# x transposed by the DMA crossbar from chunk 3 on, and a new order of a slot's work, in a windowed attention with a maxout FFN

## The chip, the cores and the metric

The kernel runs on one core of a Trainium2 chip (trn2). The metric is the device time of one execution in microseconds, the lower the better. Times of parts come from one profiled execution.

## The reference

Attention over a window of 128 positions plus four sink positions, and then a feed-forward block that takes the maximum of three products. Cut to what matters:

```python
# q, k, v: [B=4, H=8, S=768, D=64] float32
scores = scale * np.matmul(q, k.transpose(0, 1, 3, 2))
keep = (pos[None, :] < 4) | ((rel >= 0) & (rel < 128))     # rel = query - key position
a = softmax(np.where(keep, scores, -1e9))
attn = np.matmul(a, v)
x = attn.transpose(0, 2, 1, 3).reshape(B * S, H * D)       # [3072, 512]
h = np.maximum(np.maximum(x @ w1, x @ w2), x @ w3)         # [3072, 768]
out = h @ w_out                                            # [3072, 512] float32
```

## The kernel before

The 3072 tokens are worked in twelve chunks of 256 tokens (`NCH`), three to a batch (`CPB`). A chunk goes through these steps, each written as a short token in strings that `run` (L365) reads from left to right; the whole schedule is by hand (`tc.manual_schedule`, L51), so each engine executes its instructions in the order in which the tokens are written.

- `load` (L61): eight DMAs on SP's queue bring Q and K (four of 256 KB, L72) and V (four of 128 KB, L78) as float32. `cast` (L186) turns them into bf16 on POOL.
- D, `turn` (L215): two DMA transposes on SP turn K and Q of a chunk (256 KB each); used from chunk 3 on. K lands in `kT`, Q in `qT`. E, `place_k` (L192), copies `kT` on DVE into the zero-padded `kz`, in two instructions. Chunks 0 to 2 are turned on TensorE (K and Q, `prep`).
- S0 to S7, `score` (L233): for one head two or three matmuls into a PSUM tile `st` (two buffers), then an exponential on ACT (L249); every second head a multiplication by the mask on DVE (L252) for the pair. The chunk that begins a batch has no block before it, so it leaves out L240.
- Z: scores against the sinks and their exponential (L258, L263; the PSUM tile has the tag of `st`), or, on a batch's first chunk, the gathering of the batch's sink keys on DVE (L227).
- A, `av` (L268), for four heads g and 128 tokens t: matmuls with V, then on DVE a reciprocal (L285) and a product (L288) into `x_sb`.
- T0, T1, `xpose` (L293), each for 128 tokens of a chunk: four TensorE transposes of `x_sb` into PSUM (L300) and a copy by ACT into `xT` (L301).
- F0 to F8, `ffn_h` (L306): eight matmuls each with a weight block and all 256 tokens of `xT` (L313). F0, F3 and F6 (the first weight matrix) are cast on ACT into `h_sb` (L317); the others are folded in by a maximum on DVE (L319). Four PSUM buffers.
- Y0, Y1, `ffn_y` (L321): six matmuls for 128 tokens over all of `h_sb` (L324), a copy on ACT (L329), and after Y1 two stores on SP (L336).

From L442 on the loop's pass i, a slot, does D of chunk i+2, the loads and casts of chunk i+3, the attention of chunk i+1 and the feed-forward of chunk i, by this string:

```python
run("Dc", c=i + 2)
if i + 3 < NCH:
    load(i + 3)
    cast(i + 3)
run("Sb0 Fa0 Sb1 Fa1 Sb2 Fa2 Sb3 Fa3 Zb Sb4 Fa4 Ab00 Sb5 Fa5 Ab01 Sb6 Fa6 "
    "Sb7 Fa7 Fa8 Ab10 Ab11 Ec Ya0 Tb0 Tb1 Ya1", a=i, b=i + 1, c=i + 2)
```

Steps on chunks past the last are skipped: slots 9 and 10 load nothing, slot 10 has no D, and slot 11 has only F and Y. SP's queue in a slot is thus: D (two transposes), eight loads, two stores of y.

Of the kernel before, what the change touches and what calls it, by code (L numbers as in the profile page):

```python
# [10 lines left out]
BF16 = mybir.dt.bfloat16  # L11
# [5 lines left out]
def kernel(  # L17
# [13 lines left out]
    nc = tc.nc  # L31
# [10 lines left out]
    CPB = S // 256  # L42
    NCH = B * CPB
    DS = d_model // 128
# [6 lines left out]
    with tc.manual_schedule():  # L51
        const = tc.alloc_tile_pool(name="const", bufs=1)
        raw = tc.alloc_tile_pool(name="raw", bufs=3)
        work = tc.alloc_tile_pool(name="work", bufs=2)
# [6 lines left out]
        def load(ci, gate=None):  # L61

            b, c = divmod(ci, CPB)
            t0 = c * 256
            eng = nc.sync
            qk = raw.tile([128, 2, 2, 512], F32, tag="qk_raw", name="qk_raw")
            vr = raw.tile([128, 2, H, D], F32, tag="v_raw", name="v_raw")
            if gate is not None:
                gate.memset(qk[0:1, 0, 0, 0:1], 0.0)
            for g in range(2):  # L70
                for j, src in ((0, k), (1, q)):
                    eng.dma_start(  # L72
                        out=qk[:, j, g].rearrange("p (h i d) -> p h (i d)", h=4, d=D),
                        in_=src[b, 4 * g:4 * g + 4, t0:t0 + 256]
                            .rearrange("h (p i) d -> p h (i d)", i=2))
            for n in range(2):
                for i in range(2):
                    eng.dma_start(  # L78
                        out=vr[64 * i:64 * i + 64, n],
                        in_=v[b, :, t0 + 128 * n:t0 + 128 * n + 128]  # L80
                            .rearrange("h (p i) d -> i p h d", i=2)[i])
            raws[ci] = (qk, vr)
# [5 lines left out]
        for x in range(n_sink):  # L88
            nc.sync.dma_start(out=vs_raw[x * H:(x + 1) * H],
                              in_=v[:, :, x].rearrange("b h d -> h b d"))  # L90
# [35 lines left out]
        for i in range(2):  # L126
            for slot, op, sign in ((1, ALU.is_ge, 1), (0, ALU.is_gt, -1)):
                m = msk[64 * i:64 * i + 64, slot].rearrange("p (i t) -> p i t", i=2)
                nc.gpsimd.affine_select(
                    out=m, in_=m, compare_op=op, fill=0.0, base=-sign * i,  # L130
# [55 lines left out]
        def cast(ci):  # L186
            for j, g in ((0, 0), (1, 0), (0, 1), (1, 1)):
                cast_qk(ci, j, g, nc.gpsimd)
            for n in range(2):
                cast_v(ci, n, nc.gpsimd)  # L190
# [75 lines left out]
        xs = {}  # L266
# [24 lines left out]
        xTs = {}  # L291

        def xpose(ci, t):  # L293
            if t == 0:
                xTs[ci] = work.tile([128, DS, 256], BF16, tag="xT", bufs=3, name="xT")
            pt = (ps_f.tile([128, DS, 128], BF16, tag="f", name="xt_ps") if ci == 0 else
                  ps_o.tile([128, DS, 128], BF16, tag="o", name="xt_ps"))
            x = xs.pop((ci, t)).rearrange("p h d -> p (h d)")
            for ds in range(DS):
                nc.tensor.transpose(pt[:, ds], x[:, ds * 128:(ds + 1) * 128], ident)  # L300
            nc.scalar.copy(xTs[ci][:, :, t * 128:(t + 1) * 128], pt)  # L301

        hs = {}
        ys = {}
# [1 line left out]
        def ffn_h(ci, n):  # L306
            fp, wi = divmod(n, 3)
            if n == 0:
                hs[ci] = work.tile([128, FB, 256], BF16, tag="h", bufs=3, name="h_sb")
            hp = ps_f.tile([128, 2, 256], F32, tag="f", name="h_ps")  # L310
            for f in range(2):
                for ds in range(DS):
                    nc.tensor.matmul(hp[:, f], lhsT=w_sb[wi][:, ds, (2 * fp + f) * 128:(2 * fp + f + 1) * 128],  # L313
                                     rhs=xTs[ci][:, ds, :], start=(ds == 0), stop=(ds == DS - 1))
            dst = hs[ci][:, 2 * fp:2 * fp + 2]
            if wi == 0:
                nc.scalar.copy(dst, hp)  # L317
            else:
                nc.vector.tensor_max(dst, dst, hp)  # L319
# [18 lines left out]
        def step(op):  # L338

            name, ci, arg = op[0], int(op[1:3]), op[3:]  # L340
            if ci >= NCH:
                return
            if name in "KQ":
                prep(ci, int(name == "Q"), int(arg))
            elif name == "D":
                turn(ci)
            elif name == "E":
                place_k(ci, kTs.pop(ci), slice(0, NP))
            elif name == "S":
                score(ci, int(arg))  # L350
            elif name == "Z":
                if ci % CPB:
                    sink_score(ci)
                elif ci > 0:
                    sink_k(ci // CPB)
            elif name == "A":
                av(ci, int(arg[0]), int(arg[1]))
            elif name == "T":
                xpose(ci, int(arg))
            elif name == "F":  # L360
                ffn_h(ci, int(arg))
            elif name == "Y":
                ffn_y(ci, int(arg))

        def run(text, **at):  # L365
            for tok in text.split():
                c = at[tok[1]]
                step(f"{tok[0]}{c:02d}{tok[2:]}")
# [59 lines left out]
            a=0, b=1, c=2)  # L428
# [13 lines left out]
        for i in range(2, NCH):  # L442
            run("Dc", c=i + 2)
            if i + 3 < NCH:
                load(i + 3)
                cast(i + 3)
            run("Sb0 Fa0 Sb1 Fa1 Sb2 Fa2 Sb3 Fa3 Zb Sb4 Fa4 Ab00 Sb5 Fa5 Ab01 Sb6 Fa6 "
                "Sb7 Fa7 Fa8 Ab10 Ab11 Ec Ya0 Tb0 Tb1 Ya1", a=i, b=i + 1, c=i + 2)

        for pool in (ps_f, ps_o, ps_s, work, raw, const):  # L450
            pool.release()
# [35 lines left out]
```

## Time and profile before

| | |
|---|---|
| median of three runs | 211.01 us (210.33 to 216.31) |
| the profiled execution | 211.01 us, its span 209.2 us |
| mean granted TensorE clock | 0.967 |
| TensorE transposes of x (L300) | 96, 9.5 us busy |
| copies of x on ACT (L301) | 24, 13.2 us busy, 592 ns each |
| maxima (L319) | 72, 49.1 us busy on DVE |
| feed-forward matmuls (L313) | 864, 111.3 us busy |
| DMA transposes K / Q, issue to landing | 4.8 / 3.4 us, nine each |
| loads Q / K / V, issue to landing | 4.6 / 4.1 / 4.2 us |

The profile lists instructions by line and engine. PE is TensorE's matmul, PEld its weight loads, DVE, ACT and POOL the vector, scalar and GpSimd engines, SPq the queue of SyncE, which issues DMAs. "Busy" for matmuls counts overlapping pipeline time, so a row's sum is more than what it holds the array. The chain of waits is followed back from the last instruction, at each step to what released it. The loop's slots 2 to 10 fill the stretch from 61.1 to 193.9 us of the span; ahead of it lies the start with the first two chunks, after it slot 11.

### The profile page before, as it was taken

How to read it: one execution, taken by the hardware profiler on the slowest of the kernel's cores; microseconds unless marked ns; L12 is line 12 of the kernel's file. 1: busy time of each engine (PE TensorE's matmuls, PEld its weight loads, DVE VectorE, ACT ScalarE, POOL GpSimd, SP SyncE). 2: the span in 40 equal slices, each digit the busy share in tenths (PEclk: the TensorE clock that was granted, in tenths of full speed). 3: DMA queues.
4: the chain of work that ended last, by engine and by line, in shares of the span. 5: the costliest groups of instructions: out<-in, count | busy, mean ns of one | idle time of the engine just before them, and what ended most of it. 6: DMA issues, size and time to landing. Idle time of an engine off the chain costs nothing.

```text
span 209.2 us, 4734 instructions
## 1 busy us (share of the span) xinstructions
PE 187.6 (90%) x1895; PEld 149.6 (72%) x1895; DVE 122.8 (59%) x271; ACT 107.4 (51%) x198; POOL 66.6 (32%) x113
## 2 busy tenths in 40 slices
PE   7664598999839999999999999999999999999991
PEld 7544477986427959869779599599597797896860
DVE  4793340887314966737748746747768477375340
ACT  8865244154514556466375375384462853754321
POOL 7355717989005243430340421702402500000000
PEclk9999579999966999999999999999999999999999
DMA  5899995990498999939939969679489580300304
GB/s 147 226 241 197 208 253 105 202 242 1 98 231 210 196 271 189 245 82 200 265 72 151 315 115 223 168 129 278 101 162 261 128 155 3 94 9 0 100 3 100
DMA packets 75749, 33.37 MB, mean 159 GB/s; under 512 B 45776, under 2 KB 72656, under 8 KB 75728
## 3 DMA queue, kind: packets, MB, share of 16 engines
q1 hardware_dynamic: 73344, 29.93, 63.3%
q0 software_dynamic: 2384, 3.15, 8.9%
q8 instruction: 15, 0.25, 0.5%
q14 instruction: 6, 0.05, 0.1%
HBM read 25.20 MB, written 6.29 MB: 151 GB/s over the span
## 4 chain that ended last, share of the span: by engine, by line
PE 68%; DVE 11%; DMA 7%; SPq 6%; ACT 3%; issue 2%; POOL 1%; DVEq 0%; POOLq 0%
PE h_ps L313 43%; PE y_ps L324 8%; PE st L242 4%; PE o_ps L280 4%; DMA v_raw<-in_v_dram 4%; DVE x_sb L288 4%; DVE h_sb L319 4%; SPq L78 3%; DMA kT<-qk_bf 2%; PE st L243 2%; DVE e_sb L252 2%; PE xt_ps L300 2%; SPq L72 2%; PE st L240 1%; PE sk L258 1%
## 5 line engine op out<-in xcount | busy, mean ns | idle before, releaser
L313 PE MATMUL h_ps<-xT,w 128*128 128x256 bf16 x864 | 111.3, 278 | 0.7 <-ACT xT L301 0.7
L313 PEld LDWEIGHTS <-w 128*128 128x128 bf16 x864 | 82.9, 100 | 11.4 <-issue 0.8
L249 ACT ACTIVATE e_sb<-st 128x512 bf16<-128x512 f32 (+1 forms) x96 | 53.4, 564 | 33.7 <-PE st L243 32.8
L319 DVE TENSOR_TENSOR h_sb<-h_sb,h_ps 128x512 bf16<-128x512 bf16 x72 | 49.1, 683 | 22.6 <-PE h_ps L313 20.0
L252 DVE TENSOR_TENSOR e_sb<-e_sb,msk 128x1024 bf16<-128x1024 bf16 (+1 forms) x48 | 32.9, 685 | 40.8 <-ACT e_sb L249 40.6
L180 POOL CAST qk_bf<-qk_raw 128x512 bf16<-128x512 f32 x44 | 28.6, 657 | 86.7 <-DMA qk_raw<-in_k_dram 76.6
L324 PE MATMUL y_ps<-wo,h_sb 128*128 128x512 bf16 x144 | 35.3, 379 | 0.0
L329 ACT COPY y_sb<-y_ps 128x512 f32<-128x512 f32 x24 | 14.1, 586 | 37.5 <-PE y_ps L324 37.5
L242 PE MATMUL st<-qT,kz 128*128 128x256 bf16 x96 | 26.6, 281 | 5.0 <-DVE kz L196 3.9
L317 ACT CAST h_sb<-h_ps 128x512 bf16<-128x512 f32 x36 | 21.1, 586 | 15.7 <-PE h_ps L313 15.6
L243 PE MATMUL st<-qT,kz 128*128 128x128 bf16 x96 | 21.5, 225 | 0.0
L280 PEld LDWEIGHTS <-e_sb 128*128 128x128 bf16 x352 | 17.1, 99 | 6.0 <-issue 3.3
L324 PEld LDWEIGHTS <-h_sb 128*128 128x128 bf16 x144 | 12.3, 98 | 12.7 <-DVE h_sb L319 3.4
L288 DVE TENSOR_TENSOR x_sb<-o_ps,rc 128x256 bf16<-128x256 f32 x48 | 20.4, 424 | 1.6
L280 PE MATMUL o_ps<-ve,e_sb 128*128 128x65 bf16 x352 | 19.2, 196 | 0.9 <-DVE e_sb L252 0.8
L184 POOL CAST ve<-v_raw 128x512 bf16<-128x512 f32 x24 | 16.4, 694 | 10.4 <-DMA v_raw<-in_v_dram 9.9
L242 PEld LDWEIGHTS <-kz 128*128 128x128 bf16 x96 | 9.6, 100 | 6.6 <-issue 4.1
L240 PE MATMUL st<-qT,kz 128*128 128x128 bf16 x64 | 14.3, 223 | 0.0
L301 ACT COPY xT<-xt_ps 128x512 bf16<-128x512 bf16 x24 | 13.2, 596 | 0.4 <-PE xt_ps L300 0.3
L196 DVE COPY kz<-kT 64x1024 bf16<-64x1024 bf16 x18 | 9.9, 550 | 5.5 <-DMA kT<-qk_bf 5.2
L272 PE MATMUL o_ps<-vs,e_sink 128*128 128x260 bf16 x32 | 9.0, 282 | 3.4 <-POOL vs L168 3.4
L300 PE MATMUL xt_ps<-ident,x_sb 128*128 128x128 bf16 x96 | 9.5, 221 | 2.4 <-DVE x_sb L288 1.5
(44 smaller groups left out, 108.0 us busy)
## 6 DMA issues: line engine op xcount, KB each, us to landing
qk_raw<-in_k_dram SPq DMA_DIRECT2D x24, 256.0 KB, 4.1
qk_raw<-in_q_dram SPq DMA_DIRECT2D x24, 256.0 KB, 4.6
v_raw<-in_v_dram SPq DMA_DIRECT2D x48, 128.0 KB, 4.2
out_dram<-y_sb SPq DMA_DIRECT2D x22, 256.0 KB, 3.8
w<-in_moe_w_dram POOLq DMA_DIRECT2D x3, 768.0 KB, 9.4
wo<-in_moe_w_out_dram POOLq DMA_DIRECT2D x2, 384.0 KB, 5.7
out_dram<-y_sb SPq DMA_DIRECT2D x4, 128.0 KB, 2.3
kT<-qk_bf SPq DMA_TRANSPOSE x9, 4.8
```

Of the source, the lines that this page charges most:

```text
L180: eng.tensor_copy(dst.rearrange("p i (h d) -> p h i d", d=D), src)
L184: eng.tensor_copy(ve[b % 2][:, 2 * c + n, :, 0:D], raws[ci][1][:, n])
L242: nc.tensor.matmul(st[:, 1:3], lhsT=kh[:, 0:128], rhs=qh, start=True, stop=True)
L243: nc.tensor.matmul(st[:, 3], lhsT=kh[:, 128:256], rhs=qh[:, 1], start=True, stop=True)
L249: nc.scalar.activation(e[:, h, lo:], st[:, lo:], AF.Exp, scale=scale)
L252: nc.vector.tensor_tensor(out=e[:, :, lo:], in0=e[:, :, lo:], in1=m, op=ALU.mult)
L280: nc.tensor.matmul(o[:, hh], lhsT=es[ci, p][:, h, sl], rhs=ve[b % 2][:, n, 2 * p + h], start=(c == 0 and x == 0), stop=(x == len(blocks) - 1),
L288: nc.vector.tensor_mul(xs[ci, t][:, 4 * g:4 * g + 4], o[:, :, 0:D], rc.unsqueeze(2).to_broadcast([128, 4, D]))
L313: nc.tensor.matmul(hp[:, f], lhsT=w_sb[wi][:, ds, (2 * fp + f) * 128:(2 * fp + f + 1) * 128], rhs=xTs[ci][:, ds, :], start=(ds == 0), stop ...
L317: nc.scalar.copy(dst, hp)
L319: nc.vector.tensor_max(dst, dst, hp)
L324: nc.tensor.matmul(yp, lhsT=hs[ci][:, fb, t * 128:(t + 1) * 128], rhs=wo[:, fb], start=(fb == 0), stop=(fb == FB - 1))
```

## The change

From chunk 3 on, T issues one DMA transpose on SP for each half of x instead of four TensorE transposes and an ACT copy. `xT` is laid out by halves of the tokens for this, and L313 reads it in two runs of 128. The string of the loop is written anew: S1 and S2 and the later scores stand closer together, F4 to F8 come later, T0 and T1 stand directly after A10 and A11, and E stands between F6 and F7. D stands ahead of the slot's loads as it did.

```diff
@@ -292,13 +292,17 @@
 
         def xpose(ci, t):
             if t == 0:
-                xTs[ci] = work.tile([128, DS, 256], BF16, tag="xT", bufs=3, name="xT")
+                xTs[ci] = work.tile([128, 2, DS, 128], BF16, tag="xT", bufs=3, name="xT")
+            if ci >= CPB:
+                nc.sync.dma_start_transpose(
+                    out=xTs[ci][:, t], in_=xs.pop((ci, t)).rearrange("p h d -> p (h d)"))
+                return
             pt = (ps_f.tile([128, DS, 128], BF16, tag="f", name="xt_ps") if ci == 0 else
                   ps_o.tile([128, DS, 128], BF16, tag="o", name="xt_ps"))
             x = xs.pop((ci, t)).rearrange("p h d -> p (h d)")
             for ds in range(DS):
                 nc.tensor.transpose(pt[:, ds], x[:, ds * 128:(ds + 1) * 128], ident)
-            nc.scalar.copy(xTs[ci][:, :, t * 128:(t + 1) * 128], pt)
+            nc.scalar.copy(xTs[ci][:, t], pt)
 
         hs = {}
         ys = {}
@@ -311,7 +315,7 @@
             for f in range(2):
                 for ds in range(DS):
                     nc.tensor.matmul(hp[:, f], lhsT=w_sb[wi][:, ds, (2 * fp + f) * 128:(2 * fp + f + 1) * 128],
-                                     rhs=xTs[ci][:, ds, :], start=(ds == 0), stop=(ds == DS - 1))
+                                     rhs=xTs[ci][:, :, ds], start=(ds == 0), stop=(ds == DS - 1))
             dst = hs[ci][:, 2 * fp:2 * fp + 2]
             if wi == 0:
                 nc.scalar.copy(dst, hp)
@@ -444,8 +448,8 @@
             if i + 3 < NCH:
                 load(i + 3)
                 cast(i + 3)
-            run("Sb0 Fa0 Sb1 Fa1 Sb2 Fa2 Sb3 Fa3 Zb Sb4 Fa4 Ab00 Sb5 Fa5 Ab01 Sb6 Fa6 "
-                "Sb7 Fa7 Fa8 Ab10 Ab11 Ec Ya0 Tb0 Tb1 Ya1", a=i, b=i + 1, c=i + 2)
+            run("Sb0 Fa0 Sb1 Sb2 Fa1 Sb3 Zb Sb4 Fa2 Sb5 Ab00 Fa3 Sb6 Ab01 Sb7 Fa4 Fa5 Ab10 "
+                "Tb0 Ab11 Tb1 Fa6 Ec Fa7 Fa8 Ya0 Ya1", a=i, b=i + 1, c=i + 2)
 
         for pool in (ps_f, ps_o, ps_s, work, raw, const):
             pool.release()
```

## The prediction

> **What bounds the kernel now.** I read the page first (busy shares, chain), then the chain of waits in one slot, then a table of stretches with one row per slot, then the SP queue in order of time. A slot is one pass of the loop at L442.
>
> The page:
>
> ```profile
> PE 187.6 (90%) x1895; PEld 149.6 (72%) x1895; DVE 122.8 (59%) x271; ACT 107.4 (51%) x198; POOL 66.6 (32%) x113
> ...
> PE 68%; DVE 11%; DMA 7%; SPq 6%; ACT 3%; issue 2%; POOL 1%; DVEq 0%; POOLq 0%
> ```
>
> TensorE carries two thirds of the chain, yet DVE has 11%. Where, the chain in slot i=4 shows (start us, us, what):
>
> ```profile
> 101.38 0.61 ACT e_sb L249
> ...
> 102.02 0.69 DVE e_sb L252
> 102.71 0.61 DVE h_sb L319
> ...
> 103.41 0.69 DVE h_sb L319
> ...
> 104.77 0.43 DVE x_sb L288
> ...
> 105.25 0.40 PE xt_ps L300 x4
> 105.65 1.29 PE y_ps L324 x6
> ```
>
> Up to its last exponential the slot is matmul after matmul; then it is ACT, DVE and a transpose that TensorE follows. The table of stretches (window, length; busy us of PE, PEld, DVE, ACT, POOL with counts; clock; DMA share; GB/s), here slots i=2, 4 and 5:
>
> ```profile
> 61.10:77.10 16.00, 15.85 (x135) 11.89 (x135) 10.59 (x24) 6.95 (x14) 6.23 (x10) 0.85 0.99 239
> ...
> 91.90:106.80 14.90, 14.75 (x158) 12.01 (x157) 9.55 (x20) 8.57 (x16) 4.47 (x8) 1.00 0.79 177
> 106.80:120.30 13.50, 13.35 (x134) 10.49 (x133) 9.38 (x24) 7.45 (x15) 3.04 (x6) 1.00 0.97 195
> ```
>
> Slots i=2 to 10 fill 61.1 to 193.9; those that score the first chunk of a batch (i=2, 5, 8: no L240, no sink matmul) take 13.5, the others 14.8 to 15.3. The DMA engines are 0.79 to 0.99 busy wherever a slot still loads (i=2 to 8), so a new transfer meets a full path. The SP queue of slot i=4, which begins at 91.9:
>
> ```profile
> 92.71 1.30 SPq L336 DMA_DIRECT2D out_dram<-y_sb  x2
> 94.12 2.29 SPq L219 DMA_TRANSPOSE kT<-qk_bf  x1
> 96.52 1.24 SPq L219 DMA_TRANSPOSE qT<-qk_bf  x1
> 97.81 0.58 SPq L72 DMA_DIRECT2D qk_raw<-in_k_dram  x1
> ...
> 100.10 3.51 SPq L78 DMA_DIRECT2D v_raw<-in_v_dram  x4
> ```
>
> SP waits for the last y copy of the slot before, then issues without a pause until 103.6, which is **11.7 us into the slot**. Slots 5 to 8 give 11.0 to 11.6. The DMA row of the same stretch stays at 9 until about 105.4 (13.5 in); in slots 5 to 8 it drains 13.0 to 13.4 in.
>
> **What the Trainium skill says.** "DMA: Bandwidth & Descriptors", section "Queues, rings and completion order": on each DMA engine a queue's descriptors are consumed in ring order. So a transpose issued on SP after the loads moves its data after theirs; the trace agrees as far as it goes (DMA is busy without a gap until the loads have drained). "Advanced Engine Details and Errata", section "X-Bar Transpose (TRN2)", expects 350 to 400 GB/s of a transpose. The trace disagrees: from 166.0 to 171.7 two 256 KB transposes and what was left of the y stores, 1.05 MB, ran at 188 GB/s in the busy part. I use the trace. "TensorE: Matmul & The Clock Gate", section "Why this matters for your kernels", warns of TensorE gaps over about 3 us; the trace has one case, the 4 us wait ahead of slot 2, after which eight L313 matmuls took 1.71 us for 0.87.
>
> **The change, part by part.**
>
> *Removed*, chunks 3 to 11, slots 2 to 10: 72 transposes, 72 weight loads and 18 ACT copies (L301, 592 ns each). A slot's eight transposes are 8 x 0.055 = 0.44 us of matmul stream; with their waits on x_sb, TensorE spends 104.75 to 105.65 on them, **0.9 us a slot**. The copies stand beside Y1; in the steady slots nobody waits for them.
>
> *The layout of xT* makes the moving operand of L313 two runs of 128. Cost nil: L242 streams qT in four runs of 64 and its 128x256 form takes 281 ns beside L313's 278.
>
> *The order.* I walk one slot (six of nine, with sink) in the new order from these rows: S 0.22 us of stream, F 0.87, sink scores 0.44, A 0.35, Y 1.29, results 0.17 later; an exponential 0.60 and the next ACT instruction 0.49 after its start; mask and max 0.69, next after 0.61; reciprocal and product of one A 0.60; E 2 x 0.55. Clock from the slot's start; y copy at 0.20 as in the trace.
> - TensorE: S0 0, F0 0.22, S1 1.09, S2 1.33 (waits for exp 0), F1 1.55, S3 2.42, Z 2.90 (waits for exp 2), S4 3.46 (exp 3), F2 3.68, S5 4.55, A00 4.77, F3 5.12, S6 5.99, A01 6.21, S7 6.56, F4 6.78, F5 7.65, A10 8.52, A11 8.87, F6 9.22, F7 10.09, F8 10.96 to 11.83. Packed scores cost about 0.55 us of waiting for the two score buffers.
> - ACT: exp 7 ends at 7.75 (10.08 before). DVE: mask 3 at 7.78, then F4 and F5, both A products at 10.23 and 10.77, **then E until 11.85**, which now stands ahead of F7 and F8; their maxima end at 12.5 and 13.1.
> - Y0 starts at 11.83, does four of its six matmuls and waits for F8's maximum: 0.45 us. Y0 ends at 13.58, Y1 at 14.87.
>
> So the slot is 14.9 us: what the transposes gave is taken by the score buffers and by F8 behind E. The same walk without sink and L240 (mask 0.55, exp 0.49) gives 13.5, again as before. Uncertain by 0.5 down (no waits but the removed work) and 0.6 up (masks of 0.95 as at 130.4, E slowed to 1.5 as at 75.3). F6's cast sits on ACT, idle there.
>
> *The new transfers*: 18 transposes of 128 KB on SP, two a slot, behind the slot's eight loads and ahead of its two y stores. x is ready at 10.2 and 10.8, SP is free at 11.75: SP, not x, sets the issue. What is queued behind a waiting transpose (y stores, next D) waits for Y1 anyway. Issue: qT of twice the size takes 1.24, kT 2.33; half to the whole of these, I take 2.0 for the pair, so 13.75. Landing comes 2.0 after issue in qT's case (3.3 from a start of 168.77, issue 1.24): 15.75. By the DMA path: drained at 13.5, 256 KB at 188 GB/s is 1.4 us, or 2.6 if the two large transposes took all of their 5.3 us; I take 2.1, and 0.5 to the semaphore: **16.1**, bounds 15.3 and 17.0. POOL issues nothing new, and its casts wait for loads that stand ahead of the transposes.
>
> *The new wait*: F0 of the next slot reads all of xT, and TensorE is in order. It would start at 14.9 + 0.22 = 15.1, or 13.7 after a short slot. So it is late by 1.0 or 2.3. That does not add up in full: SP's next round starts at the slot's first instructions, and a slot that began F0 late has as much more time for its own transposes. Slot by slot, with s the start and d the lateness of F0:
> - i=2: loads end on SP at 76.07, drained at 78.0 (17 in, since SP was behind); xT lands near 80.5, wanted at 77.3: **d3 = 3.2**, close to the gap that cost clock before.
> - i=3: s 77.1, xT near 95, wanted 95.4: 0. i=4: s 95.2, lands 111.3, wanted 110.3: 1.0. i=5: s 110.1, 126.1 to 124.8: 1.2. i=6: s 124.6: 0. i=7: s 140.7: 1.0. i=8: s 155.6: 1.2. i=9 and 10 have no loads: 0, s 170.1 and 186.2.
> - The tail (i=11) starts at 201.1, where it was 193.9: +7.2. Slots 6 and 7 had 15.2 and 15.3 for causes on DVE that stay: +0.7. If the gap ahead of slot 3 also costs clock, as 4 us did ahead of slot 2 (2 us more on its first three F), that is worth a quarter of it here: +0.5.
>
> Sum +8.4; part of the recovery at F0 may be hidden, I take **+8**: 211 + 8 = **219 us**. The profiled execution is the 211.01 one (span 209.2, 1.8 around it) and is also the median, so nothing is rescaled.
>
> **The rivals.**
> 1. *xT late behind the loads* (above): 219; with the bounds of landing and slot length 213 to 228. For it: SP's 11.7 and DMA shares of 0.79 to 0.97. Chance 0.58.
> 2. *DVE becomes the bound*: E ahead of F7 and F8 with contention, kT late, or the maxima of F4 and F5 queued longer; slots of 15.5 to 16 and 14.3. TensorE then waits inside Y0, which hides most of the transposes' lateness: 9 x 0.9 + 3 = +11, 222 us. For it: DVE is in the chain already; against: my walk leaves only 0.45. Chance 0.19.
> 3. *The transposes land in time* (the other side): if the pair issues in 1.2 and lands 1.5 later, beside the last loads instead of behind them, xT is there at 14.5. Decisive point: landing before 14.6 in a long slot and 13.7 in a short one. With slots shortened by 0.3 to 0.7: 9 x 0.5 = -4.5, plus a first wait of 2: 208 us, at best 204. Against: the full DMA path and a short slot's 13.7. Chance 0.17, of which less than half is beyond 2%.
> 4. *The change does not do what it says*, the transposes costing SP or DMA several times their size: each slot 2 us longer, 229. The trace of D speaks against it. Chance 0.06.
>
> **The numbers.** 2% is 4.2 us, about what a measurement of this kernel can tell from no change (three runs, 210.3 to 216.3). Slower: 0.8 of case 1, nearly all of 2 and 4: 0.71; faster: 0.08; within 2%: 0.21. Range 210 to 228: it takes in the bounds of case 1, most of 2 and the dear half of 3; the likeliest case alone has 213 to 228.
>
> **What would show it.** L300 x24 and L301 x6 instead of 96 and 24; 18 transposes of x on SP starting 11 to 12 us into a slot and landing near 16; L313 waiting for a DMA xT, 3 us ahead of slot 3, then about every second slot; L324 waiting for L319 by 0.4 in each slot; ACT's copies gone. The prediction is wrong if xT lands before 14.6, if slots differ from 14.9 and 13.5 by over 0.6 without any wait for xT, or if DVE's E ends long after 11.9.

## The result and the profile after

| | |
|---|---|
| before | 211.2 us median (210.33 to 216.31) |
| changed | 224.73 us median (223.34 to 227.62) |
| ratio | 1.063, 95% interval 1.053 to 1.074: slower |
| profiled execution | 223.34 us, span 221.6 us (before 211.01 and 209.2), clock 0.958 |

Executions of one kernel spread by some per cent, so a ratio compares only the fast executions of both kernels, a median and a spread take in all of them, and where too few fast ones are left an experiment below has a median and a spread only.

The page after, busy shares and chain by engine:

```profile
PE 186.9 (84%) x1823; PEld 147.3 (66%) x1823; DVE 122.3 (55%) x271; ACT 97.6 (44%) x180; POOL 64.8 (29%) x113
...
PE 43%; SPq 17%; DVE 14%; DMA 11%; ACT 6%; issue 6%; POOL 1%; DVEq 0%; POOLq 0%
```

TensorE lost 72 matmuls and ACT 10 us of busy time (the copies), and both idle more. TensorE's share of the chain fell from 68% to 43%; SP's queue rose from 6% to 17%, DMA from 7% to 11%. The chain in slot i=4 and into slot 5 shows where (start us, us, what):

```profile
108.23 1.39 SPq L78
109.66 1.30 SPq L78
111.07 1.26 SPq L297
112.42 2.44 DMA xT<-x_sb
115.00 1.05 PE h_ps L317 x8
```

The last V loads, the two transposes of x one after the other on SP, the landing of the second, then F0 of slot 5. TensorE is not in it until F0. Waits over the whole span (who waited for whom: us, times, longest):

```profile
PEld L328 <- DVE h_sb L323: 10.6, 10, 1.7
...
PE h_ps L317 <- DMA xT<-x_sb: 7.0, 4, 3.8
...
PE y_ps L328 <- DVE h_sb L323: 5.8, 8, 1.2
```

Matmul and weight load wait beside each other, so their rows are not added. F0 waited some 7 us for xT. Y0's matmuls waited 5.8 us for the maxima of F7 and F8, about 0.6 a slot (its weight loads 10.6); in the kernel before the matmuls did not wait there at all and the weight loads 3.4. The stretches of slots 3, 4 and 5, and the first 5.6 us after slot 3's gap (window, length; busy us of PE, PEld, DVE, ACT, POOL; clock; DMA share; GB/s):

```profile
76.74:98.63 21.89, 17.25 (x150) 13.15 (x149) 10.01 (x20) 7.57 (x14) 6.61 (x10) 0.84 0.82 162
98.63:113.72 15.09, 14.56 (x150) 11.62 (x149) 9.45 (x20) 7.54 (x14) 3.42 (x6) 1.00 0.82 184
113.72:128.41 14.69, 13.04 (x125) 10.11 (x124) 9.01 (x24) 6.23 (x13) 3.09 (x6) 1.00 0.93 197
```

```profile
80.90:86.50 5.60, 5.54 (x30) 4.12 (x31) 1.40 (x3) 2.17 (x4) 0.00 (x0) 0.50 1.11 158
```

The gap itself, and F0 at half speed (1.87 us for 1.04), are in the list of TensorE's instructions (start us, us, what; in brackets the idle time just before it and what ended it):

```profile
80.96 1.87 PE L317 MATMUL h_ps<-xT,w 128*128 128x256 bf16 x8 [3.84 <-DMA xT<-x_sb]
```

Slot 3 alone took 6.9 us more than before (21.89 for 14.97): F0 came 4.0 us late, and the clock then stood at half for 5.6 us, which is 2.8 us lost. The slots agree: from F0 to its end slot 3 takes 17.7 us, slot 4, with the same work, 14.9. The difference of the spans, 12.4 us, lies as follows; lateness is the start of F0 less the slot's first score and 0.22 us (0.17 in a short slot):

| slot | before, us | after, us | of it F0 late |
|---|---|---|---|
| 2 | 15.86 | 15.04 | 0 |
| 3 | 14.97 | 21.89 | 4.0 |
| 4 | 14.88 | 15.09 | 0 |
| 5 | 13.48 | 14.69 | 1.1 |
| 6 | 15.15 | 17.09 | 1.6 |
| 7 | 15.21 | 15.50 | 0 |
| 8 | 13.47 | 15.13 | 1.0 |
| 9 | 14.89 | 15.38 | 0.3 |
| 10 | 14.88 | 14.59 | 0 |
| sum | 132.79 | 144.40 | 8.0 |

So 8.0 us are lateness of F0 (the profile puts it down to xT in every slot but 9, where it names no cause for the 0.3), 2.8 the cold clock in slot 3 (the half speed after the gap), and the rest of the loop is 0.8 us longer; the parts ahead of slot 2 and after slot 10 add the last 0.8.

### The profile page after: what moved, and what is told of

Read it like the earlier page. It is cut to its first block, busy times and chain, and to the rows that moved or that the text cites. A ratio compares the mean times of both kernels' runs of the same rounds, so it can differ in the third digit from the quotient of the medians.

```text
span 221.6 us, 4641 instructions
## 1 busy us (share of the span) xinstructions
PE 186.9 (84%) x1823; PEld 147.3 (66%) x1823; DVE 122.3 (55%) x271; ACT 97.6 (44%) x180; POOL 64.8 (29%) x113
## 4 chain that ended last, share of the span: by engine, by line
PE 43%; SPq 17%; DVE 14%; DMA 11%; ACT 6%; issue 6%; POOL 1%; DVEq 0%; POOLq 0%
PE h_ps L317 25%; PE y_ps L328 8%; DVE h_sb L323 7%; SPq L78 6%; ACT e_sb L249 5%; DMA xT<-x_sb 4%; SPq L72 4%; DMA v_raw<-in_v_dram 4%; SPq L219 3%; PE st L242 3%; PE o_ps L280 3%; DVE kz L196 2%; DVE x_sb L288 2%; DMA kT<-qk_bf 2%; SPq L297 2%
## 5 line engine op out<-in xcount | busy, mean ns | idle before, releaser
L317 PE MATMUL h_ps<-xT,w 128*128 128x256 bf16 x864 | 109.0, 279 | 7.8 <-DMA xT<-x_sb 7.0
L249 ACT ACTIVATE e_sb<-st 128x512 bf16<-128x512 f32 (+1 forms) x96 | 51.0, 565 | 21.1 <-PE st L243 21.0
L180 POOL CAST qk_bf<-qk_raw 128x512 bf16<-128x512 f32 x44 | 27.8, 637 | 98.4 <-DMA qk_raw<-in_k_dram 85.8
L328 PEld LDWEIGHTS <-h_sb 128*128 128x128 bf16 x144 | 13.1, 98 | 22.2 <-DVE h_sb L323 10.6
L243 PE MATMUL st<-qT,kz 128*128 128x128 bf16 x96 | 21.7, 228 | 0.0
L280 PEld LDWEIGHTS <-e_sb 128*128 128x128 bf16 x352 | 16.8, 99 | 6.7 <-issue 4.4
L184 POOL CAST ve<-v_raw 128x512 bf16<-128x512 f32 x24 | 14.8, 622 | 11.4 <-DMA v_raw<-in_v_dram 10.8
L242 PEld LDWEIGHTS <-kz 128*128 128x128 bf16 x96 | 9.7, 101 | 7.4 <-issue 5.1
L240 PE MATMUL st<-qT,kz 128*128 128x128 bf16 x64 | 14.6, 228 | 0.0
L196 DVE COPY kz<-kT 64x1024 bf16<-64x1024 bf16 x18 | 9.1, 508 | 5.6 <-DMA kT<-qk_bf 5.4
L285 DVE RECIPROCAL rc<-o_ps 128x4 f32<-128x4 f32 x48 | 8.4, 175 | 6.7 <-PE o_ps L280 6.7
L243 PEld LDWEIGHTS <-kz 128*128 128x128 bf16 x96 | 9.8, 102 | 2.1 <-issue 1.6
```

The costliest lines, as they stand in the source:

```text
L180: eng.tensor_copy(dst.rearrange("p i (h d) -> p h i d", d=D), src)
L184: eng.tensor_copy(ve[b % 2][:, 2 * c + n, :, 0:D], raws[ci][1][:, n])
L242: nc.tensor.matmul(st[:, 1:3], lhsT=kh[:, 0:128], rhs=qh, start=True, stop=True)
L243: nc.tensor.matmul(st[:, 3], lhsT=kh[:, 128:256], rhs=qh[:, 1], start=True, stop=True)
L249: nc.scalar.activation(e[:, h, lo:], st[:, lo:], AF.Exp, scale=scale)
L280: nc.tensor.matmul(o[:, hh], lhsT=es[ci, p][:, h, sl], rhs=ve[b % 2][:, n, 2 * p + h], start=(c == 0 and x == 0), stop=(x == len(blocks) - 1),
```

## The experiments

**Theory A**: the crossbar's x comes late because its place on SP's queue is behind a slot's loads; what costs is the wait of F0, and the cold clock after the longest one. **Theory B**: the new order costs, by packed scores and by E ahead of F7 and F8 on DVE. **Theory C**: the transfers themselves cost, because the DMA path is full. Ratios are against the kernel before on the same chip. The runs stand on four chips, on which the medians of the kernel before lie between 210.7 and 212.2 us; a comparison across them is good to 1 or 2 us. Diffs show the lines that matter (`...` stands for the rest), against the changed kernel where nothing else is said.

### The order alone, and the crossbar alone

e1 keeps the new order and gives x back to TensorE; e2 keeps the old order and has the crossbar.

```diff
e1:
-            if ci >= CPB:
+            if ci >= NCH:
...
-                "Tb0 Ab11 Tb1 Fa6 Ec Fa7 Fa8 Ya0 Ya1"
+                "Ab11 Fa6 Ec Fa7 Fa8 Ya0 Tb0 Tb1 Ya1"
e2:
-            run("Sb0 Fa0 Sb1 Sb2 Fa1 Sb3 Zb ... Ya0 Ya1"
+            run("Sb0 Fa0 Sb1 Fa1 Sb2 Fa2 Sb3 Fa3 Zb ... Ec Ya0 Tb0 Tb1 Ya1"
```

> New order of the slot, x transposed on TensorE as before (T0 and T1 between Y0 and Y1, E still between F6 and F7). Theory A (SP order: the crossbar's x comes late because it is issued on SP behind a slot's loads; that is 8 us of waits ahead of F0 and 3 us of cold clock in slot 3): the order alone costs little, about 0.4 us a slot, 215 us. Theory B (the new order itself, DVE with E ahead of F7 and F8, is what costs): 220 us or more.

> Old order, x transposed by the crossbar with T where it was, between Y0 and Y1. Theory A: x is ready only 13.3 us into the slot, the pair lands near 16.5, wanted at 14.2, in every slot and not in every second one: 225 us, with waits of L317 on the DMA of xT in all nine slots. Theory B: 211 to 214 us.

e1 took 217.89 us (216.0 to 218.76), ratio 1.029, 1.021 to 1.038: between the two theories. The order costs 6 us when TensorE still does the transposes, and its profile shows where: Y0's matmuls wait 5.7 us for the maxima, which they did not before. e2 took 237.68 (233.85 to 241.03), ratio 1.114, 1.099 to 1.129. Its waits:

```profile
PE h_ps L317 <- DMA xT<-x_sb: 22.4, 9, 3.5
```

Nine waits in nine slots, 2.5 us each, as theory A has it: in the old order x is ready late in the slot, and being late then repeats in each. The expectation of 225 was still 12 too low. Most of that is clock: after five of the nine gaps (2.25 to 3.46 us) TensorE ran at half clock for a while, some 1.6 us lost each time; after the other four (2.21 to 2.38 us) it did not. The mean clock of its executions was 0.914 to 0.949, that of the kernel before 0.954 to 0.983. So the new order is what makes the crossbar bearable, and it has its own price.

### The transfers without the wait

The cleanest test of theory C: all 18 crossbar transposes are issued, into tiles that nobody reads, and F reads TensorE's copy. e11 does so in e1's order, e12 in the order of before; the strings are shown against those two.

```diff
+        def spare(ci, t):
+            xd = work.tile([128, DS, 128], BF16, tag="xD", bufs=4, name="xD")
+            nc.sync.dma_start_transpose(out=xd, in_=xs[ci, t].rearrange("p h d -> p (h d)"))
e11:
-                "Ab11 Fa6 Ec Fa7 Fa8 Ya0 Tb0 Tb1 Ya1"
+                "Xb0 Ab11 Xb1 Fa6 Ec Fa7 Fa8 Ya0 Tb0 Tb1 Ya1"
e12:
-                "Sb7 Fa7 Fa8 Ab10 Ab11 Ec Ya0 Tb0 Tb1 Ya1"
+                "Sb7 Fa7 Fa8 Ab10 Ab11 Ec Ya0 Xb0 Xb1 Tb0 Tb1 Ya1"
```

> The kernel of the order-only run with 18 crossbar transposes of x added at the places of the changed kernel, into tiles that nobody reads; F reads the TensorE copy. So SP and the DMA engines carry all that the change puts on them, and no F0 waits for it. Theory A (it is the wait of F0 that costs): as the order-only run, 217 to 219 us. Theory C (the traffic costs, by delaying D, the loads and the y stores): 221 us or more.

> The kernel before with the same 18 unread crossbar transposes, issued on SP between Y0 and T0 of each slot. Theory A: 211 to 213 us, against 234 to 241 with the same transfers read by F0. Theory C: 220 us or more.

e11: 217.11 us (215.34 to 217.32), beside 217.89 for e1 on another chip. e12: 208.47 us (205.9 to 210.23), with 212.15 (207.09 to 214.17) for the kernel before on its chip; its median is the lower one and the two spreads overlap, so it is no slower, and not shown to be faster. The same transfers read by F0 had cost 26 us in e2. SP's queue of e12 in one slot, and its slots 4 and 5 in the columns of the table of stretches:

```profile
101.89 2.69 SPq L78 DMA_DIRECT2D v_raw<-in_v_dram  x4
104.68 2.56 SPq L309 DMA_TRANSPOSE xD<-x_sb  x2
```

```profile
91.39:106.27 14.88, 14.68 (x157) 11.98 (x157) 9.80 (x20) 8.57 (x16) 4.42 (x8) 1.00 1.04 203
106.27:119.75 13.48, 13.28 (x133) 10.45 (x133) 9.73 (x24) 7.44 (x15) 3.64 (x6) 1.00 1.07 214
```

The transposes take their 2.56 us on SP behind the loads, the DMA share rises from 0.79 and 0.97 to 1.04 and 1.07, and the two slots are as long as in the kernel before, 14.88 and 13.48. **Theory C falls: at this place on SP the transfers cost nothing that shows; waiting to read them does.** e12 also has the new layout of `xT`, so that layout costs nothing either.

### Where x stands on SP, and where E stands

e4 moves the four V loads of a slot to POOL's queue; e5 leaves them on SP and puts them (`load_v`), and their casts on POOL (`cast_v`), behind T1; e3 puts E behind F8; e6 is e5 and e3 together. a0 is the changed kernel again, beside e5 and e6.

```diff
e4:
-                load(i + 3)
+                load(i + 3, veng=nc.gpsimd)
e3:
-                "Tb0 Ab11 Tb1 Fa6 Ec Fa7 Fa8 Ya0 Ya1"
+                "Tb0 Ab11 Tb1 Fa6 Fa7 Fa8 Ec Ya0 Ya1"
e5 (e6 with "Fa6 Fa7 Fa8 Ec Ya0 Ya1"):
+                load(i + 3, late_v=True)
+                cast(i + 3, late_v=True)
...
+                "Tb0 Ab11 Tb1", a=i, b=i + 1, c=i + 2)
+            if i + 3 < NCH:
+                load_v(i + 3)
+                for n in range(2):
+                    cast_v(i + 3, n, nc.gpsimd)
+            run("Fa6 Ec Fa7 Fa8 Ya0 Ya1", a=i, b=i + 1, c=i + 2)
```

> The changed kernel with the four V loads of each slot issued from POOL's queue instead of SP's, the same bytes. SP is then free 2.7 to 4.1 us earlier. Theory A: the transposes of x start when x is ready (about 10.5 us into the slot) and land near 13.5 to 14; the waits ahead of F0 go, slot 3's gap and its cold clock too: 213 to 215 us. Theory C (the DMA path itself is full, so the data of x moves late wherever it is issued): 222 to 225 us.

> The changed kernel with E after F8 instead of between F6 and F7; nothing else moved. Theory A: the 0.7 us wait inside Y0 goes in each slot, but where xT is late F0 then waits as much longer, so only part of it shows: 221 us. Theory B: the full 9 x 0.7 us, 218 us or less.

> The changed kernel once more, so that the three others have it measured on the same chip: 223 to 228 us.

> The changed kernel with the four V loads of a slot (and their casts) put behind T1 on SP's queue; Q, K and D stay ahead, all bytes stay. Theory A (place on SP): SP is free 8 us into the slot, x's transposes start at 10.5 when x is ready and land at 13.0 to 14.2, ahead of the F0 that reads them; slot 3's gap goes too, with its cold clock: 213 to 216 us. Theory C (the DMA path is full in total): what x gains V loses, V pushes the next slot's D and loads later, 220 us or more.

> As the run with x ahead of V, and E after F8 as well. Theory A with the DVE share of theory B: the wait inside Y0, 0.7 us a slot, now shows in full since no transposed x covers it: 6 us less than that run, 207 to 210 us, at or under the kernel before. If the transposes of x still bind, it is the same as that run.

e4 missed: 226.12 us (220.18 to 231.66), a wide spread, and no gain that shows in it. In its profile, of the execution of 231.66 us, SP was free earlier, as meant, but POOL's loads now ran beside D:

```profile
101.88 2.06 SPq L219 DMA_TRANSPOSE kT<-qk_bf  x1
104.03 3.52 SPq L219 DMA_TRANSPOSE qT<-qk_bf  x1
```

```profile
DVE kz L196 <- DMA kT<-qk_bf: 11.1, 4, 5.5
```

Q's transpose holds SP for 3.5 us instead of 1.25, and K lands 9.3 us after its issue at the median, where it was 4.9. So E waits for K (four times, 11.1 us, where it was once, 5.4), and behind E on DVE stand the maxima of F7 and F8 (longest wait of Y0 3.8 us, where it was 1.2). F0's waits for xT did shrink, from 7.0 to 3.8 us: what x gained, D lost. Theory A took the places on SP for the whole story; in this trace, loads that another queue issues beside a transpose on SP slow it.

e3 gave 222.5 us with 216.96 to 225.61: too wide for a verdict alone. F0's waits for xT rose from 7.0 to 10.7 us, and Y0's matmuls no longer waited (its weight loads 4.1 us for 10.6), as expected of two waits that cover each other.

e5 took 217.71 us (215.66 to 219.21), ratio 1.025, 1.015 to 1.035, beside a0's 225.7 (222.26 to 226.62), ratio 1.057. Eight us by moving four loads behind two transposes, with all bytes kept. The gap ahead of slot 3 fell to 1.6 us, and the clock stayed up, as F0's 1.03 us show:

```profile
78.50 1.03 PE L325 MATMUL h_ps<-xT,w 128*128 128x256 bf16 x8 [1.60 <-DMA xT<-x_sb]
```

e6 took 213.7 (212.21 to 217.24), ratio 1.007, 0.998 to 1.016: some 4 us more by moving E. SP's queue of e6:

```profile
101.19 0.51 SPq L72 DMA_DIRECT2D qk_raw<-in_q_dram  x1
102.92 2.89 SPq L305 DMA_TRANSPOSE xT<-x_sb  x2
105.86 2.70 SPq L86 DMA_DIRECT2D v_raw<-in_v_dram  x4
```

SP now waits for x (from 101.7 to 102.9) instead of x for SP. Both expectations were 2 to 4 us too good: three waits for xT are left in e6, since a transpose of x there takes 2.8 us at the median and up to 4.1 to land, 2.4 at best. That the Q and K loads still in flight do this is likely, but no run shows it.

### The first gap

e7 lets TensorE transpose x of chunk 3 only, to take slot 3's gap and cold clock away.

```diff
-            if ci >= CPB:
+            if ci >= CPB + 1:
```

> The changed kernel with x of chunk 3 alone transposed on TensorE. This takes the 4 us gap ahead of slot 3 and the cold clock after it (3 us) away, and puts some 2 us of TensorE waits on x into slot 2: 5 us less than the changed kernel on the same chip. If the gap only hides other waiting (the queue of slot 2), less than 2.

It gave 224.61 us with 218.66 to 228.46, no clear gain over a0's 225.7. The matmuls of its profile, of the execution of 228.46 us, show why:

```profile
95.39 1.90 PE L328 MATMUL y_ps<-wo,h_sb 128*128 128x512 bf16 x8 [0.42 <-DVE h_sb L323]
99.50 1.66 PE L317 MATMUL h_ps<-xT,w 128*128 128x256 bf16 x8 [2.00 <-DMA xT<-x_sb]
101.81 1.70 PE L317 MATMUL h_ps<-xT,w 128*128 128x256 bf16 x8
```

Slot 3 is on time, and so slot 4 is the late one, and slots 6 and 8 after it: F0 waits for xT, and the next F groups run at half speed (1.70 us for 1.04). Slot 2, where TensorE now waits to transpose x, takes 18.3 us for 15.0. A gap taken away at its first place moves to the next, because its cause stands in each slot. That is a miss of the expectation.

### A version with what was learnt

e8: x ahead of V, E behind F8, scores packed less, and slot 2 as before with x of chunk 3 on TensorE. e9: the same less packed order in every slot, with all x on TensorE and the loads undivided.

```diff
e8:
+            run("Sb0 Fa0 Sb1 Fa1 Sb2 Sb3 Fa2 Zb Sb4 Fa3 Sb5 Ab00 Sb6 Ab01 Fa4 Sb7 Fa5 Fa6 "
+                "Ab10 Tb0 Ab11 Tb1", a=i, b=i + 1, c=i + 2)
...
+            run("Fa7 Fa8 Ec Ya0 Ya1", a=i, b=i + 1, c=i + 2)
e9:
+                "Ab10 Ab11 Fa7 Fa8 Ec Ya0 Tb0 Tb1 Ya1", a=i, b=i + 1, c=i + 2)
```

> A version that keeps what the runs showed to be good: x ahead of V on SP, E after F8, scores packed less (S and F alternate except S2 with S3; S6, A01, F4, S7), and the crossbar only from chunk 4, with slot 2 as in the kernel before (x of chunk 3 on TensorE). Walked with the rows of the profile a long slot is 14.0 us, 0.8 under the kernel before; if the crossbar's x still lands in time at 13.9: 204 to 206 us. If the transposes run into the Q and K loads (4.1 us to landing at worst in the last run), F0 waits again: 209 to 212 us.

> The same less packed order with E after F8, but all x transposed on TensorE between Y0 and Y1 and the loads undivided as before; no crossbar for x. It tells what the crossbar itself brings once it is not late: TensorE has 0.44 us more a slot and no transfer to wait for. 207 to 209 us; if the order alone is the gain, the same as the run before.

In 22 executions e8's median was 210.23 us (206.71 to 214.21), ratio 1.000, 0.987 to 1.014, so no gain is seen. e9's was 210.01 (205.02 to 212.17); its ratio is 0.977, 0.971 to 0.983, but rests on three executions against five, and the medians of all, 22 against the kernel before's 43 at 210.7, lie 0.3% apart. Whether e9 gains anything is not settled. In e8 F0 still waits for xT 5.0 us in all (longest 2.3); e9 has no such wait. Where e8's x is in time its slots take 14.33 and 13.15 us, e9's 14.78 and 13.60: the 0.45 us a slot are there to be had, about what the eight transposes stream. Three late slots (15.0, 16.1 and 16.8) take them back.

## Why the prediction was right, and where its sizes were off

The direction and the mechanism of the likeliest case (rival 1) held: xT late behind the loads on SP. Measured +12.4 us of span (+13.5 between the medians), foretold +8; the range of 210 to 228 took the 224.7 in. That the landing came out right is in part luck.

- **The place on SP.** Foretold: SP free at 11.75, pair issued in 2.0, landed at 16.1. Measured in slot 4: the first transpose 12.4 us into the slot, 2.56 for the pair, landed at 16.2. Three sizes were off and cancelled: SP was free 0.6 later (the V loads held it 4.1 us, not 3.5), the issue was 0.56 longer, and the landing came 1.2 us after the end of issue in place of 2.35.
- **The DMA path.** I had x's data wait for the loads to drain and take 2.1 us more. It doesn't. The DMA row of the changed kernel, here from 108 to 116 us in steps of 0.2, falls to 0.3 to 0.4 between 111.2 and 112.0, just after x's first transpose was issued at 111.07:

```profile
DMA  8989999999999999433489999510799300000008
```

In slot 9, which loads nothing, the pair goes no faster:

```profile
186.96 2.50 SPq L297 DMA_TRANSPOSE xT<-x_sb  x2
```

There the second transpose lands 2.4 us after its issue, as in slots 2, 4 and 5 behind loads; from first issue to last landing the pair takes 3.6 us, in those three slots 3.8 to 4.1. The loads ahead cost x its place on SP, and on the path at most 0.5 us. The chain of waits in slot 4, from the V loads' issue to that of x to its landing, and e12 say the same. The Trainium skill's ring order ("DMA: Bandwidth & Descriptors", "Queues, rings and completion order") is not contradicted, but it was not what bound. The DMA share of 0.79 to 0.97 was read as a path with no room, and it had room.
- **Lateness slot by slot.** Foretold 3.2, 0, 1.0, 1.2, 0, 1.0, 1.2, 0 for slots 3 to 10; measured 4.0, 0, 1.1, 1.6, 0, 1.0, 0.3, 0. Held, 7.6 against 8.0 in sum, but for slot 9. There the amount changes from one execution to the next: a0, the same kernel, has 4.3, 0, 0.8, 1.2, 0.4, 0, 3.2, 0, which is 9.9.
- **The cold clock**, the term that was mis-sized most: "a quarter of it here: +0.5". It measured 2.8 us. A lateness of 4.0 us (3.84 of it idle) was followed by half clock for 5.6 us, much as the 4 us ahead of slot 2 had been before, for 4.9 us. In a0 the gap ahead of slot 3 cost 1.7 us, and the one of 3.0 ahead of F0 in slot 9 again 1.7. The skill's "TensorE: Matmul & The Clock Gate", "Why this matters for your kernels", warns of gaps over about 3 us, and the walk itself gave a gap of 3.2: it should have been priced in full. e7 shows half clock after its own gap of 2.0 in slot 4 too; in e5, with a gap of 1.6, slot 3's matmuls ran at full speed. Rewritten with the 2.8, the sum is 10.7 instead of 8.4.
- **The order.** Foretold: packed scores and E ahead of F7 and F8 eat the 0.9 us of the transposes, slots of 14.9 and 13.5. Measured without lateness: 15.1 in slot 4 and 13.6 in slot 5, but 15.5 in slots 6 and 7 and 14.1 in slot 8, where Y0 waits 0.8 to 1.2; that is at the edge of the 0.6 which the prediction allowed. Of the parts, Y0's wait was 0.42 in slot 4 and 0.6 a slot over all, where 0.45 was foretold, and e6 against e5 prices E's place at some 4 us for nine slots, which is 0.45. e1 says the same from the other side: with TensorE transposing as well, the order costs 6 us, 0.7 a slot.
- **Rival 2** (DVE) is thus true in part, as a second wait that xT's lateness partly covers; **rival 3** (in time) needed x ahead of V (e5); with E moved as well (e6), and with three waits for xT still left, it gave a tie.

## What to carry to other kernels

Moving a step from a busy engine to a transfer trades its busy time for a latency plus the transfer's place in the issuing queue: work out at what time in the loop its input is ready, when the queue is free, and when the first reader stands there. To tell a transfer's cost from the cost of waiting for it, issue it into a tile that nobody reads. A TensorE gap that comes near the length after which the trace has already shown a cold clock is priced with that clock.

## What the runs showed of the hardware

- In the changed kernel a crossbar transpose of 128 partitions by 512 bf16 holds SP's queue for 1.19 to 1.58 us and lands 2.4 us after its issue at the median, 3.5 at most. Of D's two, of twice the size, the first holds SP 2.3 us and the second 1.24.
- Loads moved from SP's queue to POOL's made the transposes on SP slower, though the bytes stayed the same: in slots 3 to 8 of e4's profile the second of D's two held SP for 2.9 to 4.3 us, and K landed after 9.3 us at the median instead of 4.9.
- In the loops of these traces half clock followed every TensorE gap of 3.0 us or more (3.0 in a0, 3.8 in the changed kernel). After gaps of 2.0 to 2.7 us it came at times (2.0 in e7, 2.25 in e2, 2.7 in e4) and at times not (2.35 and 2.38 in e2), so no single length decides it here. Gaps up to 1.6 us (e5) left the clock up. Half clock lasted up to 5.6 us.
